# One slot later for the second projection, two conversion pieces at other slots, and differences one step ahead, in a two-layer MLP kernel on one Trainium2 core

## Chip, core and metric

The kernel runs on one core of one Trainium2 chip. The metric is the device time of one execution in microseconds; a kernel's time is the median of its runs. The engines are PE (TensorE; its weight loads are listed apart as PEld), DVE (VectorE), ACT (ScalarE), POOL (GpSimd) and SP (SyncE, which here issues nearly all DMAs).

## What is computed

Attention with random features gives `x` of 2304 tokens by 512 features. Two MLP layers follow, each 512 to 2048 to 512 in fp32:

```python
# layer 1
h = x @ w_in
g = h - np.tanh(h)
x = (g @ w_out)
# layer 2
h = x @ w_in
g = h * (1.0 / (1.0 + np.exp(-1.702 * h)))
out = (g @ w_out)
```

Weights arrive as 64-bit floats, and the kernel converts them itself. Every fp32 operand of a product is split into a high part and a low part (`two`: ACT casts `hi`, then POOL or DVE subtracts to get `lo`), and a product is three passes, hi·hi, hi·lo, lo·hi.

## The kernel before

The program has three stages: attention (with the first conversions of layer 1's weights), layer 1, and layer 2. All engines work through their instructions in program order, so the order in which the source emits instructions is the schedule.

**Layer 2** (from line 848 on) is cut into 24 groups: three blocks of 768 tokens (`sb` 0, 1, 2) by eight weight pairs `j`. `GROUPS` runs blocks 0 and 1 alternately over j = 0 to 7 (groups 0 to 15), then block 2 over j = 7 to 0 (groups 16 to 23). The first product of a group is done with seven products instead of eight, over sums and differences of 2x2 blocks: seven prepared forms of x (`xform`, P1 to P7) times seven prepared forms of the weights (`win`). Their results accumulate in PSUM banks: `a` (P1, P6, P5, P3 in this order), `c` (P7, P4) and `b` (P2). Between the products of a bank, `vec` copies or adds what the bank holds at that moment: `h_add` (line 864) makes `hx` on DVE, `keep` (line 868) a copy on ACT. So P6 in slot 2 can't start before the `hx` of G11, issued in slot 0, has read bank `a`.

A group has seven slots. In each slot PE gets one of the first products (`h_slot`; 6 matmuls) and one or two pieces of the second projection of the group before (`y_chunk`; 6 matmuls each, eight pieces (t, d) per group, placed by `YS`). A piece needs all of `g` for its half t of the tokens: G11 and G21 for t = 0, G12 and G22 for t = 1. `g` is made by ACT (sigmoid), DVE (multiply), ACT (cast to hi) and POOL (lo, line 886). `y_chunk` ends with a DVE addition into `yacc` (line 847), which stands on DVE's queue ahead of the slot's `vec` work.

**Conversion in layer 2.** For the pairs j = 3 to 7, groups 4 to 13 also convert weights. A pair takes two groups (an even and an odd one), and `L2_TICKS` says at which slot of which a piece runs: `a`, `b`, `c`, `d` convert a raw tile (two ACT instructions, then the DVE instructions of lines 289 and 294), `b`, `c`, `d` also split an earlier part into hi and lo on ACT and POOL; `s` makes four sums on DVE (line 451); `h`, `o`, `e` split on ACT and POOL.

**Forms of x.** `xprep_ticks` prepares the seven forms of a block in the order P2, P1, P7, P6, P4, P5, P3, in steps k = 0 to 6 for both halves kt. Steps 1 to 4 start with a difference on DVE (line 526), then `two` casts the source on ACT and subtracts on POOL (kt = 0) or DVE (kt = 1). Block 0 is prepared during layer 1, block 1 in groups 0 and 1, block 2 in groups 14 and 15.

**Layer 1** runs 36 steps per half of its hidden features; `y` lives in four PSUM banks which `evac` (line 402) adds up on DVE at the end of a token block, and the next block's `y_mm` waits for that.

Of the kernel before, what the change touches and what calls it, by code (L numbers as in the profile page):

```python
# [15 lines left out]
ALU = mybir.AluOpType  # L16
# [30 lines left out]
NPAIR = NF // 2  # L47
NPRE = 3
GROUPS = [(sb, j) for j in range(NPAIR) for sb in range(2)] + [(2, j) for j in reversed(range(NPAIR))]
NG = len(GROUPS)  # L50

L1_TICKS = ("a", "b", "s", "ch", "d", "oe")
L2_TICKS = {(0, 1): "a", (0, 5): "b", (0, 6): "s", (1, 1): "c", (1, 3): "h", (1, 5): "d", (1, 6): "o", (2, 0): "e"}
SLOTS = ("P1", "P7", "P6", "P4", "P5", "P2", "P3")
XID = dict(P2=0, P1=1, P7=2, P6=3, P4=4, P5=5, P3=6)
WID = dict(P1=0, P2=1, P7=2, P6=3, P5=4, P3=5, P4=6)
# [3 lines left out]
def body(ctx, tc, qT, kT, v, om, w1, w2, out):  # L60
    nc = tc.nc
# [445 lines left out]
    def xprep_ticks(sb, tiles, place):  # L507
        xi = {}

        def load():  # L510
            u = tiles(4)
            for kt in range(2):
                b1, b2 = tiles(2 * kt), tiles(2 * kt + 1)
                xi[kt] = b1, b2, u[:, kt, :]
                for i in range(2):
                    nc.sync.dma_start(
                        out=(b1, b2)[i],
                        in_=ysf[2 * i + kt, :, sb * 2 * TW:(sb + 1) * 2 * TW].rearrange("p (a c) -> p a c", c=TW))

        def tick(kt, k):  # L520
            b1, b2, t1 = xi[kt]
            b11, b12, b21, b22 = b1[:, 0, :], b1[:, 1, :], b2[:, 0, :], b2[:, 1, :]
            sums = {1: (t1, b12, b11), 2: (b12, b22, b12), 3: (b11, b22, t1), 4: (b21, b21, b11)}
            if k in sums:
                o, x, y = sums[k]
                nc.vector.tensor_tensor(out=o, in0=x, in1=y, op=ALU.subtract)
            src, i = ((b21, "P2"), (b11, "P1"), (b12, "P7"), (b11, "P6"), (b21, "P4"), (t1, "P5"), (b22, "P3"))[k]
            i = XID[i]
            v = place(i)[:, kt] if place else rp.tile([128, 2, TW], F32R, tag="xo", name="xo", bufs=4)
            two(v[:, 0, :], v[:, 1, :], src, (nc.gpsimd, nc.vector)[kt])  # L530
            if not place:
                store(xf[i, :, kt * 2 * TW:(kt + 1) * 2 * TW].rearrange("p (a c) -> p a c", c=TW), v.bitcast(F32))

        return load, [lambda kt=kt, k=k: tick(kt, k) for k in range(7) for kt in range(2)]

# [316 lines left out]
    def ya_tile(name):  # L852
        return l2.tile([128, 2, TW], F32, tag="yacc", name=name, bufs=8)

    YS = (((0, 0),), ((0, 1),), ((0, 2),), ((0, 3), (1, 0)), ((1, 1),), ((1, 2),), ((1, 3),))

    hx, sv, sg, gt = {}, {}, {}, {}

# [84 lines left out]
    for n in range(NG + 1):  # L943
        sb, j = GROUPS[min(n, NG - 1)]
        for s in range(7):
            flush()
            if n < NG and (n or s > 1):
                h_slot(n, s)
            if n:
                for t, d in YS[s]:  # L950
                    y_chunk(n - 1, t, d)
            if n < NG or s < 2:
                vec(n, s)
            if n == 0 and s == 1:
                evac(*ev, 0)
                load_win(1)
                load_wout(1)
            if n == NG:
                continue
            if s == 0 and n > 1:  # L960
                if sb == 0 and 1 <= j < NPAIR - 1:
                    (load_win if j + 1 < NPRE else new_w)(j + 1)
                elif sb == 2 and 0 < j < NPAIR - 1:
                    load_win(j - 1)
            if s == 6 and n > 1:
                if sb == 0 and 1 <= j < NPAIR - 1:
                    (load_wout if j + 1 < NPRE else new_wo)(j + 1)
                elif sb == 2 and 0 < j < NPAIR - 1:
                    load_wout(j - 1)
            q = n * 7 + s  # L970
            if xticks:
                if 3 <= q < 98 or q > 100:
                    xticks.popleft()()
                    xticks.popleft()()
            elif n == 1 and s == 4:
                begin, ts = conv_ticks(l2, range(NPRE, NPAIR), place)
                begin()
                ticks.extend(ts)
            if ticks:
                at = q - 7 * (2 * NPRE - 2)  # L980
                for x in L2_TICKS.get((at // 7 % 2, s), "") + (L2_TICKS.get((2, s), "") if at >= 14 and at // 7 % 2 == 0 else ""):
                    if at >= 0 and ticks[0][0] == x:
                        ticks.popleft()[1]()
            if n == 14 and s == 0:
                assert not ticks
                flush()

                def x2_tile(i):
                    if i == 4:
                        return l2.tile([128, 2, TW], F32, tag="ssum", name="xi", bufs=1)  # L990
                    return cv.tile([128, 2, TW], F32, tag=("raw", "ye")[i % 2], name="xi", bufs=2)

                xload, xt = xprep_ticks(2, x2_tile, lambda i: xform[2, i])
                xload()
                xticks.extend(xt)
                new_x2(2, 0)
            if n == 14:
                if SLOTS[s] != "P2":
                    new_x2(2, XID[SLOTS[s]])
# [48 lines left out]
```

## Time and profile before

| | us |
|---|---|
| median of 3 runs | 941.35 (939.5 to 942.11) |
| profiled execution, its own time | 941.45 |
| its span, first to last instruction | 939.7 |
| PE busy / PEld busy | 906.5 (96%) / 820.2 (87%) |
| DVE / ACT / POOL busy | 640.9 (68%) / 563.6 (60%) / 464.3 (49%) |

The profiled execution is 0.1 us above the median, and 1.75 us of it lie outside its span. A row of a timeline gives the start, the time from start to end, engine, source line, operation, tiles, and in brackets how long the engine was idle before it and what ended that. PE rows overlap, since matmuls are pipelined.

### The profile page before, as it was taken

How to read it: one execution, taken by the hardware profiler on the slowest of the kernel's cores; microseconds unless marked ns; L12 is line 12 of the kernel's file. 1: busy time of each engine (PE TensorE's matmuls, PEld its weight loads, DVE VectorE, ACT ScalarE, POOL GpSimd, SP SyncE). 2: the span in 40 equal slices, each digit the busy share in tenths (PEclk: the TensorE clock that was granted, in tenths of full speed). 3: DMA queues.
4: the chain of work that ended last, by engine and by line, in shares of the span. 5: the costliest groups of instructions: out<-in, count | busy, mean ns of one | idle time of the engine just before them, and what ended most of it. 6: DMA issues, size and time to landing. Idle time of an engine off the chain costs nothing.

```text
span 939.7 us, 14423 instructions
## 1 busy us (share of the span) xinstructions
PE 906.5 (96%) x5192; PEld 820.2 (87%) x5192; DVE 640.9 (68%) x1041; ACT 563.6 (60%) x1175; POOL 464.3 (49%) x361
## 2 busy tenths in 40 slices
PE   8999999999999999999989989999999998999998
PEld 6888877888898888888878879989989988999998
DVE  5999988756666656778656385577787777544454
ACT  5888878777777767777556453355554554333332
POOL 3555534556656656776746352244454565222222
PEclk9999999999999999999999999999999999999999
DMA  6787854033354242668655863034533111353542
GB/s 208 230 263 245 261 189 160 23 135 101 103 201 131 93 135 83 228 230 321 229 208 211 349 258 123 1 114 144 168 124 121 59 51 43 114 197 149 221 152 84
DMA packets 56248, 151.83 MB, mean 162 GB/s; under 512 B 6384, under 2 KB 13168, under 8 KB 53872
## 3 DMA queue, kind: packets, MB, share of 16 engines
q1 hardware_dynamic: 56032, 150.57, 46.7%
q8 instruction: 41, 0.67, 0.3%
q10 hardware_dynamic: 144, 0.33, 0.1%
q14 instruction: 31, 0.25, 0.1%
HBM read 104.48 MB, written 46.40 MB: 161 GB/s over the span
## 4 chain that ended last, share of the span: by engine, by line
PE 71%; DVE 12%; ACT 6%; POOL 5%; issue 4%; DMA 2%; SPq 0%; POOLq 0%; ACTq 0%; DVEq 0%
PE y L381 17%; PE hs L837 16%; PE hs L343 16%; PE y L816 13%; PE y L200 3%; PE y L183 2%; DVE raw L294 2%; PE y L124 1%; DVE ssum L451 1%; DVE yacc L847 1%; POOL wq L371 1%; DVE wq L373 1%; PE hs L152 1%; DVE hx L864 1%; DMA wfi<-stg 1%
## 5 line engine op out<-in xcount | busy, mean ns | idle before, releaser
L837 PE MATMUL hs<-g,wout 128*128 128x384 f32 x1152 | 229.1, 336 | 9.3 <-POOL g L886 8.5
L837 PEld LDWEIGHTS hs<-g,wout 128*128 128x128 f32 x1152 | 201.5, 188 | 13.4 <-POOL g L886 12.3
L343 PE MATMUL hs<-xb,w 128*128 128x512 f32 (+1 forms) x960 | 211.1, 371 | 1.5 <-DVE t L372 1.5
L816 PE MATMUL y<-x,win 128*128 128x384 f32 x966 | 195.0, 336 | 8.0 <-DVE hx L864 6.3
L381 PE MATMUL y<-ghi,w 128*128 128x512 f32 (+1 forms) x640 | 194.1, 371 | 4.3 <-DVE ye L402 4.3
L343 PEld LDWEIGHTS hs<-xb,w 128*128 128x128 f32 x960 | 168.6, 190 | 32.1 <-DVE t L372 1.7
L886 POOL TENSOR_TENSOR g<-sg,g 128x384 fp32r<-128x384 f32 x96 | 104.7, 1091 | 181.8 <-ACT g L885 177.0
L816 PEld LDWEIGHTS y<-x,win 128*128 128x128 f32 x966 | 169.4, 188 | 11.5 <-DVE hx L864 7.4
L357 POOL TENSOR_TENSOR glo<-wq,ghi 128x512 fp32r<-128x512 f32 x72 | 100.3, 1394 | 140.5 <-ACT ghi L355 140.5
L847 DVE TENSOR_TENSOR yacc<-hs,yacc 128x384 f32<-128x384 f32 x168 | 92.6, 554 | 100.0 <-PE hs L837 99.9
L373 DVE COPY_PREDICATED wq<-m,t 128x512 f32<-128x512 uint16 x72 | 86.1, 1196 | 106.1 <-POOL wq L371 105.0
L381 PEld LDWEIGHTS y<-ghi,w 128*128 128x128 f32 x640 | 117.9, 191 | 25.1 <-issue 5.2
L381 PE MATMUL y<-glo,w 128*128 128x512 f32 (+1 forms) x320 | 118.6, 371 | 0.0
L876 ACT ACTIVATE sg<-hx 128x384 f32<-128x384 f32 x72 | 37.8, 526 | 114.5 <-DVE hx L864 106.6
L885 ACT CAST g<-sg 128x384 fp32r<-128x384 f32 x96 | 49.4, 515 | 91.4 <-DVE sg L879 91.4
L371 POOL TENSOR_TENSOR wq<-wq,s 128x512 f32<-128x512 f32 x70 | 90.6, 1294 | 18.6 <-DVE wq L370 17.6
L134 POOL PARTITION_ALL_REDUCE mq<-pq x32 | 65.9, 2107 | 61.2 <-ACT pq L132 61.2
L363 ACT ACTIVATE s<-hs 128x512 f32<-128x512 f32 x72 | 42.9, 596 | 62.0 <-PE hs L343 61.9
L381 PEld LDWEIGHTS y<-glo,w 128*128 128x128 f32 x320 | 61.1, 191 | 10.0
L370 DVE SCALAR_TENSOR_TENSOR wq<-wq,hs 128x512 f32<-128x512 f32 x72 | 49.1, 682 | 18.6 <-ACT t L365 18.6
L355 ACT CAST ghi<-wq 128x512 fp32r<-128x512 f32 x72 | 44.3, 615 | 26.0 <-DVE wq L373 26.0
L364 ACT ACTIVATE wq<-s,qb 128x512 f32<-128x512 f32 x72 | 52.3, 726 | 7.2 <-POOL glo L357 0.6
(119 smaller groups left out, 1280.4 us busy)
## 6 DMA issues: line engine op xcount, KB each, us to landing
raw<-w SPq DMA_DIRECT2D x57, 512.0 KB, 4.4
xb<-xs SPq DMA_DIRECT2D x24, 512.0 KB, 5.6
win<-wfi SPq DMA_DIRECT2D x9, 1280.0 KB, 8.4
wout<-wfo SPq DMA_DIRECT2D x9, 1024.0 KB, 4.8
xf<-xo SPq DMA_DIRECT2D x14, 384.0 KB, 3.5
x<-xf SPq DMA_DIRECT2D x7, 768.0 KB, 12.3
vt<-v SPq DMA_DIRECT2D x16, 325.0 KB, 3.4
kt<-kT SPq DMA_DIRECT2D x15, 320.0 KB, 3.4
```

The source lines that it names most:

```text
L134: nc.gpsimd.partition_all_reduce(mqs[i, j], pq[:, j, :], channels=128, reduce_op=bass.bass_isa.ReduceOp.max)
L343: nc.tensor.matmul(h[:, j * n:j * n + n], w[:, 0, a, kt * 128:kt * 128 + 128], x[:, c, kt, :n], start=(k == 0), stop=(k == 11))
L357: nc.gpsimd.tensor_tensor(out=lo, in0=g, in1=hi.bitcast(F32), op=ALU.subtract)
L364: nc.scalar.activation(out=w, in_=s, func=AF.Square, scale=QS, bias=qb)
L371: (nc.vector if si < 2 else nc.gpsimd).tensor_tensor(out=w, in0=w, in1=s, op=ALU.mult)
L373: nc.vector.copy_predicated(out=w, mask=m.bitcast(mybir.dt.uint16), data=t)
L381: nc.tensor.matmul(y[d][:, :n], w[:, 1, a, d * 128:d * 128 + 128], g[c][:, j * n:j * n + n], start=(first and j == 0 and k == 0), stop=(la ...
L816: nc.tensor.matmul(dst, w[:, WID[name], a, kt * 128:kt * 128 + 128], xt[:, kt, c, :], start=(first and k == 0), stop=(k == 5), skip_group_ ...
L837: nc.tensor.matmul(dst, wout[j][:, f, a, d * 128:d * 128 + 128], gt[n, f, t][:, c, :], start=(k == 0), stop=(k == 5))
L847: nc.vector.tensor_tensor(out=u, in0=dst, in1=u, op=ALU.add)
L885: nc.scalar.copy(out=u[:, 0, :], in_=g)
L886: nc.gpsimd.tensor_tensor(out=u[:, 1, :], in0=g, in1=u[:, 0, :].bitcast(F32), op=ALU.subtract)
```

## The change

The pieces of the second projection move by one slot: an entry of `YS` now names how many groups back it works, so that slot 0 does the last piece of the group before the previous one, and slots 1 to 6 the other seven of the previous group. The load of `wout` moves with them from slot 6 to slot 0 of the next group. In `L2_TICKS`, `s` moves from slot 6 of the even group to slot 1 of the odd one, and `c` from slot 1 to slot 2. In `xprep_ticks` the difference that step k + 1 needs is made at the end of step k.

```diff
-L2_TICKS = {(0, 1): "a", (0, 5): "b", (0, 6): "s", (1, 1): "c", (1, 3): "h", (1, 5): "d", (1, 6): "o", (2, 0): "e"}
+L2_TICKS = {(0, 1): "a", (0, 5): "b", (1, 1): "s", (1, 2): "c", (1, 3): "h", (1, 5): "d", (1, 6): "o", (2, 0): "e"}
...
-            if k in sums:
-                o, x, y = sums[k]
-                nc.vector.tensor_tensor(out=o, in0=x, in1=y, op=ALU.subtract)
             src, i = ((b21, "P2"), (b11, "P1"), (b12, "P7"), (b11, "P6"), (b21, "P4"), (t1, "P5"), (b22, "P3"))[k]
...
+            if k + 1 in sums:
+                o, x, y = sums[k + 1]
+                nc.vector.tensor_tensor(out=o, in0=x, in1=y, op=ALU.subtract)
...
-    YS = (((0, 0),), ((0, 1),), ((0, 2),), ((0, 3), (1, 0)), ((1, 1),), ((1, 2),), ((1, 3),))
+    YS = (((2, 1, 3),), ((1, 0, 0),), ((1, 0, 1),), ((1, 0, 2), (1, 0, 3)), ((1, 1, 0),), ((1, 1, 1),), ((1, 1, 2),))
...
-            if n:
-                for t, d in YS[s]:
-                    y_chunk(n - 1, t, d)
+            for m, t, d in YS[s]:
+                if n >= m:
+                    y_chunk(n - m, t, d)
+            if n == NG and s == 6:
+                y_chunk(n - 1, 1, 3)
...
+            if s == 0 and n > 2:
+                at = GROUPS[n - 1]
+                if at[0] == 0 and 1 <= at[1] < NPAIR - 1:
+                    (load_wout if at[1] + 1 < NPRE else new_wo)(at[1] + 1)
+                elif at[0] == 2 and 0 < at[1] < NPAIR - 1:
+                    load_wout(at[1] - 1)
...
-            if s == 6 and n > 1:
-                if sb == 0 and 1 <= j < NPAIR - 1:
-                    (load_wout if j + 1 < NPRE else new_wo)(j + 1)
-                elif sb == 2 and 0 < j < NPAIR - 1:
-                    load_wout(j - 1)
```

**PE, the start of an odd group that converts** (L816 with `win` is a first product, two rows of L837 are one piece of the second projection; `g_6933` and `g_6998` are t = 0 of the group before, the other `g` are t = 1). Before:

```order
L816 MATMUL y_7011<-x_5597,win 128x384 x6
L837 MATMUL hs<-g_6933,wout 128x384 x3
L837 MATMUL hs<-g_6998,wout 128x384 x3
L816 MATMUL y_7032<-x_5598,win 128x384 x6
L837 MATMUL hs<-g_6933,wout 128x384 x3
L837 MATMUL hs<-g_6998,wout 128x384 x3
L816 MATMUL y_7011<-x_5599,win 128x384 x6
```

In the change the tiles are numbered anew: `g_6925` and `g_6990` are t = 0 of the group before, `g_6879` and `g_6851` t = 1 of the one before that.

```order
L816 MATMUL y_6995<-x_5597,win 128x384 x6
L837 MATMUL hs<-g_6879,wout 128x384 x3
L837 MATMUL hs<-g_6851,wout 128x384 x3
L816 MATMUL y_7017<-x_5598,win 128x384 x6
L837 MATMUL hs<-g_6925,wout 128x384 x3
L837 MATMUL hs<-g_6990,wout 128x384 x3
L816 MATMUL y_6995<-x_5599,win 128x384 x6
```

The first piece that reads the new t = 0 stands behind P7 instead of behind P1; between P1 and P6 there is one of its pieces, not two.

**DVE, from the end of an even group that converts into the odd one** (L289 and L294 belong to piece `b`, later ones to `c`; L451 is `s`; `hx<-..,sp` is G11 of the odd group). Before:

```order
L294 SCALAR_TENSOR_TENSOR raw_6380<-raw_6380 128x512
L847 TENSOR_TENSOR yacc<-hs,yacc 128x384
L879 TENSOR_TENSOR sg<-hx,sg 128x384
L451 TENSOR_TENSOR ssum<-raw_6380 128x256
L451 TENSOR_TENSOR ssum<-raw_6331,raw_6380 128x256
L451 TENSOR_TENSOR ssum<-ssum,raw_6331 128x256
L451 TENSOR_TENSOR ssum<-raw_6331,ssum 128x256
L847 TENSOR_TENSOR yacc<-hs,yacc 128x384
L864 TENSOR_TENSOR hx<-y_6672,sp 128x384
L879 TENSOR_TENSOR sg<-y_6502,sg 128x384
L847 TENSOR_TENSOR yacc<-hs,yacc 128x384
L289 SCALAR_TENSOR_TENSOR raw_6499<-raw_6499 128x512
```

In the change:

```order
L294 SCALAR_TENSOR_TENSOR raw_6389<-raw_6389 128x512
L847 TENSOR_TENSOR yacc<-hs,yacc 128x384
L880 TENSOR_TENSOR sg<-hx,sg 128x384
L847 TENSOR_TENSOR yacc<-hs,yacc 128x384
L865 TENSOR_TENSOR hx<-y_6656,sp 128x384
L880 TENSOR_TENSOR sg<-y_6494,sg 128x384
L847 TENSOR_TENSOR yacc<-hs,yacc 128x384
L451 TENSOR_TENSOR ssum<-raw_6389 128x256
L451 TENSOR_TENSOR ssum<-raw_6366,raw_6389 128x256
L451 TENSOR_TENSOR ssum<-ssum,raw_6366 128x256
L451 TENSOR_TENSOR ssum<-raw_6366,ssum 128x256
L847 TENSOR_TENSOR yacc<-hs,yacc 128x384
```

The four sums leave their place in front of `hx` and stand behind it, one slot on.

**DVE in layer 1, up to the addition that frees the PSUM banks of `y`** (L526 and L532 are the differences, L423 the low part of the x form for kt = 1). Before:

```order
L373 COPY_PREDICATED wq<-m,t 128x512 [waits DVE_49,Activation_49,Pool_49]
L526 TENSOR_TENSOR xi<-xi 128x384 x2
L423 TENSOR_TENSOR xo<-xi,xo 128x384 [waits DMAHW0_49,Activation_49]
L402 TENSOR_TENSOR ye<-y_4420,ye 128x512 [waits DMAHW7_49,PE_49]
L402 TENSOR_TENSOR ye<-y_4421,ye 128x512 [waits PE_49]
```

In the change:

```order
L373 COPY_PREDICATED wq<-m,t 128x512 [waits DVE_49,Activation_49,Pool_49]
L532 TENSOR_TENSOR xi<-xi 128x384
L423 TENSOR_TENSOR xo<-xi,xo 128x384 [waits DMAHW0_49,Activation_49]
L532 TENSOR_TENSOR xi<-xi 128x384
L402 TENSOR_TENSOR ye<-y_4420,ye 128x512 [waits DMAHW7_49,PE_49]
L402 TENSOR_TENSOR ye<-y_4421,ye 128x512 [waits PE_49]
```

The cast that L423 waits for no longer needs a difference of the same step; the two differences here are those of the step after.

## Rows read from the trace of the kernel before

**Rows 1.** PE in a stretch of windows (engines' busy us and counts, PEclk, DMA, GB/s)

```profile
800.00:926.00 126.00, 125.93 (x727) 125.61 (x726) 63.20 (x124) 41.96 (x90) 32.28 (x32) 1.00 0.41 158
```

**Rows 2.** Waits by engine, layer 2: us in total, times, longest

```profile
PE hs L837 <- POOL g L886: 8.5, 12, 1.0
...
PEld hs L837 <- POOL g L886: 12.3, 12, 1.3
```

**Rows 3.** The chain that ended last, in order of time: start us, us, what

```profile
604.81 1.04 PE y L816 x6
...
613.96 1.74 DVE raw L294
...
750.57 1.71 DVE raw L294
```

**Rows 4.** Timeline of PE in one pair of converting groups

```profile
615.05 0.86 PE L837 MATMUL hs<-g,wout 128*128 128x384 f32 x4
616.61 0.61 PE L837 MATMUL hs<-g,wout 128*128 128x384 f32 x2 [0.70 <-POOL g L886]
...
620.12 1.31 PE L816 MATMUL y<-x,win 128*128 128x384 f32 x6 [0.79 <-DVE hx L864]
...
634.18 0.62 PE L837 MATMUL hs<-g,wout 128*128 128x384 f32 x2 [0.62 <-POOL g L886]
```

**Rows 5.** Timeline of POOL at the same place

```profile
613.83 1.32 POOL L423 TENSOR_TENSOR win<-raw,win 128x512 fp32r<-128x512 f32 x1 [5.57 <-ACT win L422]
615.11 1.45 POOL L886 TENSOR_TENSOR g<-sg,g 128x384 fp32r<-128x384 f32 x1
...
621.54 1.02 POOL L886 TENSOR_TENSOR g<-sg,g 128x384 fp32r<-128x384 f32 x1 [2.69 <-ACT g L885]
```

**Rows 6.** Timeline of DVE at the same place

```profile
605.00 0.69 DVE L294 SCALAR_TENSOR_TENSOR raw<-raw 128x512 int32<-128x512 int32 x1
...
616.09 0.88 DVE L879 TENSOR_TENSOR sg<-hx,sg 128x384 f32<-128x384 f32 x1
616.89 0.41 DVE L451 TENSOR_TENSOR ssum<-raw 128x256 f32<-128x256 f32 x1
...
618.01 1.12 DVE L451 TENSOR_TENSOR ssum<-raw,ssum 128x256 f32<-128x256 f32 x1
...
619.52 0.54 DVE L864 TENSOR_TENSOR hx<-y,sp 128x384 f32<-128x384 f32 x1
```

**Rows 7.** Timeline of layer 1 where PE waits for the addition of `y`

```profile
470.55 0.98 ACT L422 CAST xo<-xi 128x384 fp32r<-128x384 f32 x2 [4.47 <-DVE xi L526]
...
477.11 1.01 DVE L526 TENSOR_TENSOR xi<-xi 128x384 f32<-128x384 f32 x2
...
479.60 2.47 DVE L402 TENSOR_TENSOR ye<-y,ye 128x512 f32<-128x512 f32 x4
...
480.43 0.36 PE L381 MATMUL y<-ghi,w 128*128 128x256 f32 x1 [4.33 <-DVE ye L402]
```

**Rows 8.** Windows around that wait and around a shorter one

```profile
476.00:484.00 8.00, 3.67 (x19) 3.60 (x19) 6.21 (x10) 3.81 (x7) 3.92 (x4) 0.80 0.22 79
...
550.00:556.00 6.00, 3.73 (x20) 3.34 (x20) 5.42 (x10) 1.50 (x4) 3.34 (x3) 1.00 1.01 376
```

**Rows 9.** Start of layer 2: its window, and a PE wait of the timeline

```profile
538.00:562.00 24.00, 19.72 (x102) 17.50 (x101) 19.83 (x30) 12.77 (x29) 13.00 (x12) 1.00 0.68 253
...
555.07 1.28 PE L816 MATMUL y<-x,win 128*128 128x384 f32 x6 [1.26 <-DVE hx L864]
```

**Rows 10.** Timeline of PE in groups 14 and 15

```profile
787.59 0.61 PE L837 MATMUL hs<-g,wout 128*128 128x384 f32 x2 [0.93 <-POOL g L886]
...
791.46 1.32 PE L816 MATMUL y<-x,win 128*128 128x384 f32 x6 [1.15 <-DVE hx L864]
```

**Rows 11.** SP's timeline in block 2, and the landing of `win` from its tile's view

```profile
835.08 0.32 SPq L714 DMA_DIRECT2D wout<-wfo  x1
835.45 0.90 SPq L708 DMA_DIRECT2D win<-wfi  x2
...
DMA to landing us min/median/max: 3.9/6.2/10.0
```

## The prediction

> **What bounds the kernel.** PE does, and the question is only where it still waits. The first view is the windows: in the late stretch of layer 2 PE and its weight loads are busy for all but a fraction of 126 us [rows 1], so nothing can be won there. The second view is the list of waits: over layer 2 PE waits twelve times for POOL's low part of g before a piece of the second projection [rows 2]. The third is the chain of waits in order of time. Where PE is not disturbed, six matmuls follow each other in 1.04 us [rows 3]; so a group of 7 first products and 8 pieces should take 15 x 1.04 = 15.6 us and a pair of groups 31.2. But in the stretch that converts weights the DVE instruction of line 294 recurs in the chain from 613.96 to 750.57 [rows 3], four pairs in 136.61 us, 34.15 each. So a converting pair loses 2.95 us.
>
> The timeline names the three places of that loss [rows 4]: the first piece of the second projection stops in the middle for the low part of G21 (616.61, and 634.18 in the next group), and P6 waits for hx (620.12). The same three repeat in all five pairs, fifteen waits. The other places where PE waits are one in layer 1 [rows 7], the start of layer 2 [rows 9], and groups 14 and 15 [rows 10]. A busier DVE costs nothing until PE waits for it.
>
> **How much one wait costs.** The rows of PE in one pair give 0.70 + 0.79 + 0.62 = 2.11 us idle [rows 4], while the period says 2.95. Over layer 2 the twelve waits are 8.5 us of idle PE but 12.3 us of idle weight loading [rows 2]: the PE rows carry modelled ends that cover part of the gap. I take the period, since it is elapsed time. The Trainium skill (Perfetto Trace Analysis, Identifying the Most-Contended Engine) calls matmul busy time a bad measure of distance to the bound, since matmuls are pipelined, and wants the weight loads' busy share; by PE's rows the five pairs would give 5 x 2.11 = 10.6 us, by the period 14.8. The trace sides with that page here.
>
> **Term 1, the converting groups.** *The low part of G21.* POOL works on a split of `win` (1.32 us) when the cast of G21 is ready, and its low part ends at 615.11 + 1.45 = 616.56 [rows 5]. The first piece started at 615.05 [rows 4] and ran four of six matmuls before it needed that. In the change P7 and a piece of older data come first: P1, old piece, P7, then the new piece at 615.05 + 2 x 1.04 = 617.13, which is past 616.56 before its first matmul. Both such waits of a pair go, and the pieces for t = 1 get a slot more as well. *P6 and hx.* Today the four sums run from 616.89 to 618.01 + 1.12 = 619.13, and hx comes after them, from 619.52 to 620.06 [rows 6]; P6 starts at 620.12. Without the sums the queue reads: multiplication until 616.97, one y addition (as long as the hx row, some 0.46 from start to start), hx from about 617.35 to 617.89. The old piece it adds ended at 615.05 + 1.04 = 616.09, so that addition is not late. P6 would be free to start at 615.05 + 3 x 1.04 = 618.17. It is met with 0.28 us to spare. *What is late next.* The sums (2.24 us) and the conversion of `c` (0.69 + 0.69 alone, 1.74 for the second where POOL is in the way [rows 3, 6]) now stand in slots 1 to 3 of the odd group, with four y additions, a multiplication and one hx at about 0.54: 6.9 to 7.9 us of DVE work in 7 x 1.04 = 7.28 us. DVE ends those slots at most 0.6 us late; the next product that waits for DVE is P3 in slot 6, two slots on, and the y pieces rotate through four PSUM buffers. ACT's casts and POOL's low parts behind the moved pieces keep a slot of room. So all three waits go: **5 x 2.95 = 14.8 us**. Ends: 14.8, and 7.4 if hx becomes a new wait (first rival).
>
> **Term 2, layer 1.** In one place PE stands 4.33 us for the addition of y (480.43), because DVE's queue has the x form in front: two differences at 477.11, then a low part that waits for ACT's cast, then the additions at 479.60 [rows 7]. ACT had waited 4.47 us for the differences a step earlier too (470.55) [rows 7], and the next step's activations stood behind that cast. With differences one step ahead the casts don't wait. Walking the queues on with row durations, the step before starts its activations some 3 us earlier, of which DVE's own work takes back a part, and the additions start near 477.0 instead of 479.6: **2.6 us**. Ends: 0.6 (only the last cast's wait goes) and 4.3. After the 4.33 us of idling the granted clock was at its lower level for a while: 0.80 on the mean of the 8 us around it, which is 0.2 x 8 = 1.6 us of full-clock work; after an idle time of 1.26 us it stayed at 1.00 [rows 8]. What remains of the wait, about 1.7 us, is nearer to the 1.26, so I count the **1.6 us** as won, with 0 as the low end.
>
> **Term 3, start of layer 2.** PE is busy 19.72 of 24 us there [rows 9], so 4.3 us can be won at most. But DVE is busy 19.83 of those 24 and works through the same differences, low parts and hx; they only change places, and one difference now stands before an hx of slot 4. P6 of group 1, which waited 1.26 us until 555.07 [rows 9], has one piece fewer before it and would start at some 553.9. That piece, 1.04 us, is done at the end of the kernel instead. Net **0.9 us**, ends -1 and 4.3.
>
> **Term 4, groups 14 and 15.** The wait for g at 787.59 (0.93) goes as in term 1. The wait for hx at 791.46 (1.15) [rows 10] shrinks little: the differences stay on DVE ahead of hx, only the stop for ACT's cast between them goes. I count **1.5 us**, ends 0 and 3.1.
>
> **At no cost.** The number of matmuls, DVE, ACT and POOL instructions and DMAs is unchanged. The last piece now follows after the loop, in a tail of PE work that is as long as what it left out earlier. The `wout` load is issued a slot later, behind a piece of slot 0, and `win` of the same slot behind it on SP; PE's cover for it is priced as the last rival. The `s` and `c` pieces issue their loads of raw weights one slot later; these are read seven slots on.
>
> Sum: 14.8 + 2.6 + 1.6 + 0.9 + 1.5 = 21.4 us, from the profiled execution's own 941.45 (its median stands 0.1 lower): **920.0 us**.
>
> **Rivals.**
>
> *hx is a new wait (chance 0.13).* The margin of 0.28 us in term 1 is the thinnest in the change. Line 294 took 0.69 us where POOL was idle and 1.74 us begun beside a POOL split [rows 3, 5, 6]. If one more low part of g, 1.02 us [rows 5], falls before hx at each of the ten group starts, each loses 1.02 - 0.28 = 0.74 us, 7.4 in all: 927.4 us. For it speaks that the moved pieces meet other POOL work than now; against it, that the instructions ahead of hx are the ones that stand there today, with their delays in my numbers. The Trainium skill (SBUF — State Buffer, Who interferes with whom) says that a DVE instruction with two SBUF inputs and a GpSimd one that reads SBUF exclude each other for the whole instruction, whichever came first; by that rule this rival is what happens wherever the two meet ahead of hx. The trace agrees with it at 613.96.
>
> *Everything goes (0.10).* The upper ends of all terms: 14.8 + 4.3 + 1.6 + 4.3 + 3.1 = 28.1 us, 913.4 us. Against it stands DVE's load at the start of layer 2.
>
> *Nothing comes of it (0.04).* The waits return elsewhere, since `g` is as late as before and only its reader moved: within 0.3% (2.8 us, about what a measurement can tell) of 941.4. A reader that moves by two products, 2.08 us, against waits of at most 1.3 us [rows 2] speaks against it.
>
> *Slower: the weights of block 2 come late (0.03).* `wout` now waits for the piece of slot 0 and `win` stands behind it on SP. Today both go at 835.08 and 835.45 [rows 11]; the change puts `win` at about 837.5. It must be there for P2 in slot 5, at 835.0 + 11 x 1.04 = 846.4. The slowest landing, 10.0 us [rows 11], would give 848, but that is the larger second part, which is read two slots later still. From 846.4 on each us late costs PE one us in each of six groups; to eat 21.4 us and 3 more, the load must be 4 us late in all six, a landing of 13 us, and the time would be above 944. No row shows such a landing.
>
> **How the numbers follow.** Forecast 0.70. The range takes in the forecast with the ends of its terms, the first rival and the second: 912 to 930. Outside are the last two rivals and rest of the tails. Faster by over 0.3%: 0.70 + 0.13 + 0.10 = 0.93; within: 0.04; slower: 0.03.
>
> **What would show it.** Right: no wait of PE on POOL's g in the converting groups, a pair's period near 31.2 us, the layer 1 wait under 2.6 us with a clock of 1.00 after it, no wait in block 2. Wrong: fifteen waits of about a us at other lines, or P6 waiting for hx in most converting groups; a wait of 4 us left in layer 1; PE waiting on `win` after 835.

## The result and the profile after

The changed kernel takes 933.68 us (median of 4 runs, 932.13 to 933.95), the kernel before 941.73 (4 runs, 939.5 to 942.5): ratio 0.9915, 95% interval 0.9895 to 0.9935. It is faster by some 8 us, where 21.4 were forecast, and lies above the upper end of the range (930). The profiled execution took 933.93 us with a span of 932.1, against 939.7 before.

The account below (7.6 us, against 7.5 between the spans) is taken between starts of the same matmuls in both traces (in layer 2 what is left after 0.1733 us, a sixth of 1.04, for each matmul of the stretch, since one piece of the second projection has moved from its start to its end).

| stretch | forecast, us won | measured, us won |
|---|---|---|
| up to layer 1's wait | 0 | -0.6 |
| layer 1's wait and the rest of layer 1 | 4.2 | -1.1 |
| start of layer 2 (groups 0 and 1) | 0.9 | -4.3 |
| converting groups 4 to 13, and group 14 | 14.8 | 13.1 |
| group 15 | 1.5 | 0.5 |
| rest | 0 | 0.0 |
| sum | 21.4 | 7.6 |

Group 14 stands with the converting groups because the fifteenth of the waits that the prediction counted there is in its slot 0. The first row is chance: in both traces the 16 matmuls of line 152 that start at 5.64 us run the same code, and take 2.08 us here and 1.50 before; over the runs below the same 16 take 1.16 to 2.08.

**The converting groups did what was forecast.** In the page's group of the second projection PE no longer waits for `g` (the 12 waits of [rows 2] are gone):

```profile
L837 PE MATMUL hs<-g,wout 128*128 128x384 f32 x1152 | 226.2, 335 | 0.0
```

In the chain of waits (start us, us, what) the same work of a pair now recurs every 31.54 us, (737.06 - 610.90) / 4, where it was 34.15 [rows 3]; 31.2 was forecast:

```profile
610.90 2.08 PE hs L837 x12
...
737.06 2.08 PE hs L837 x12
```

What is left is one short stop of P6 for `hx` at the start of groups 6, 8, 10, 12 and 14, 0.26 us each (0.52 in group 10). In group 6 two sixes of matmuls take 640.12 - 637.78 = 2.34 instead of 2.08. PE's timeline, and DVE's with what stands ahead of that `hx` (the last instruction of a converted piece, 1.67 us beside a POOL split, and a multiplication of 0.90):

```profile
637.78 1.21 PE L837 MATMUL hs<-g,wout 128*128 128x384 f32 x6
638.97 1.31 PE L816 MATMUL y<-x,win 128*128 128x384 f32 x6
640.12 1.20 PE L837 MATMUL hs<-g,wout 128*128 128x384 f32 x6
```

```profile
635.02 1.67 DVE L294 SCALAR_TENSOR_TENSOR raw<-raw 128x512 int32<-128x512 int32 x1
...
637.09 0.90 DVE L880 TENSOR_TENSOR sg<-hx,sg 128x384 f32<-128x384 f32 x1
...
638.37 0.54 DVE L865 TENSOR_TENSOR hx<-y,sp 128x384 f32<-128x384 f32 x1
```

**The waits that are left** (PE; us in total, times, longest) stand in layer 1 and at the start of layer 2, and they have grown:

```profile
PE y L381 <- DVE ye L402: 5.2, 1, 5.2
PE y L816 <- ACT x L422: 2.9, 1, 2.9
PE y L816 <- DVE hx L865: 2.8, 2, 2.6
```

The first was 4.33 [rows 7]. The second is P6 of group 1; it was 1.26 [rows 9]. The view names ACT's cast there, because it ended last by the profile, but the timeline shows `hx` ending at that moment (557.29 + 0.54 = 557.83, PE starts at 557.98). The 2.6 of the third line is in group 15.

**Layer 1.** DVE's timeline ahead of the additions of `y`, then POOL's:

```profile
477.28 1.50 DVE L373 COPY_PREDICATED wq<-m,t 128x512 f32<-128x512 uint16 x1 [0.86 <-POOL wq L371]
478.68 0.54 DVE L532 TENSOR_TENSOR xi<-xi 128x384 f32<-128x384 f32 x1
479.14 0.54 DVE L423 TENSOR_TENSOR xo<-xi,xo 128x384 fp32r<-128x384 f32 x1
479.61 1.61 DVE L532 TENSOR_TENSOR xi<-xi 128x384 f32<-128x384 f32 x1
481.15 2.47 DVE L402 TENSOR_TENSOR ye<-y,ye 128x512 f32<-128x512 f32 x4
```

```profile
477.20 0.99 POOL L423 TENSOR_TENSOR xo<-xi,xo 128x384 fp32r<-128x384 f32 x1
479.51 1.30 POOL L357 TENSOR_TENSOR glo<-wq,ghi 128x512 fp32r<-128x512 f32 x1 [1.31 <-ACT ghi L355]
```

The casts do not hold DVE up any more, as intended. But the predicated copy now starts 0.08 us after a POOL subtraction and takes 1.50 us, and the second difference starts 0.10 us after another and takes 1.61 instead of 0.54. So the additions start at 481.15 instead of 479.60 [rows 7]; 0.6 of that is the first row of the table, and 0.9 is the growth of the wait.

Such instructions had two durations before as well. DVE's timeline there, the predicated copy three steps ahead of the additions, a low part, and the copy of the last step:

```profile
458.38 1.55 DVE L373 COPY_PREDICATED wq<-m,t 128x512 f32<-128x512 uint16 x1 [2.52 <-POOL wq L371]
...
465.63 1.64 DVE L423 TENSOR_TENSOR xo<-xi,xo 128x384 fp32r<-128x384 f32 x1
...
476.49 0.73 DVE L373 COPY_PREDICATED wq<-m,t 128x512 f32<-128x512 uint16 x1 [1.83 <-POOL wq L371]
```

Over the whole kernel the same 24 differences cost DVE 22.4 us instead of 13.3 (groups of lines; busy, mean ns). Before, and then after:

```profile
L526 DVE TENSOR_TENSOR xi<-xi 128x384 f32<-128x384 f32 x24 | 13.3, 595 | 0.0
```

```profile
L532 DVE TENSOR_TENSOR xi<-xi 128x384 f32<-128x384 f32 x24 | 22.4, 933 | 0.0
```

**Start of layer 2.** DVE's timeline, POOL's, and PE's:

```profile
552.06 1.35 DVE L423 TENSOR_TENSOR x<-xi,x 128x384 fp32r<-128x384 f32 x1
553.34 1.36 DVE L532 TENSOR_TENSOR xi<-xi 128x384 f32<-128x384 f32 x1
...
556.02 1.34 DVE L532 TENSOR_TENSOR xi<-xi 128x384 f32<-128x384 f32 x1
557.29 0.54 DVE L865 TENSOR_TENSOR hx<-y,sp 128x384 f32<-128x384 f32 x1
```

```profile
551.68 1.32 POOL L887 TENSOR_TENSOR g<-sg,g 128x384 fp32r<-128x384 f32 x1
552.96 1.32 POOL L423 TENSOR_TENSOR x<-xi,x 128x384 fp32r<-128x384 f32 x1
555.79 1.17 POOL L887 TENSOR_TENSOR g<-sg,g 128x384 fp32r<-128x384 f32 x1 [1.50 <-ACT g L886]
```

```profile
557.98 2.26 PE L816 MATMUL y<-x,win 128*128 128x384 f32 x6 [2.85 <-ACT x L422]
```

A difference or a low part that meets a POOL subtraction takes 1.35 us here, and POOL's own take 1.32 instead of 1.02. Four of the eight differences from 545 to 557 us are held so, and all eight stand ahead of `hx`. The `hx` itself, with one of its two inputs in PSUM, takes 0.54 although POOL runs another subtraction from 556.91 to 558.23. The windows (busy us and counts of PE, PEld, DVE, ACT, POOL; PEclk) show what the wait then cost beyond itself:

```profile
538.00:562.00 24.00, 18.14 (x82) 15.73 (x81) 18.23 (x26) 12.53 (x28) 12.61 (x11) 0.90 0.69 260
...
561.00:563.00 2.00, 2.00 (x8) 2.00 (x8) 0.80 (x2) 0.58 (x2) 1.56 (x2) 0.50 0.04 8
```

PE is busy 1.58 us less than before (18.14 against 19.72 [rows 9]), and it then works at the lower of its two clock levels (0.50, 1.2 of 2.4 GHz) until some 564.0: from 557.98 that is 6.0 us, in which half as much is done, 3.0 us. Together 4.6, about the 4.3 of the table. Block 2 has no waits, as before [rows 1]: PE is again busy 125.93 of the 126 us from 800 on.

### The profile page after: what moved, and what is told of

Same layout as the page of the kernel before. It is cut to its first block, busy times and chain, and to the rows that moved or that the text cites. A ratio compares the mean times of both kernels' runs of the same rounds, so it can differ in the third digit from the quotient of the medians.

```text
span 932.1 us, 14425 instructions
## 1 busy us (share of the span) xinstructions
PE 906.5 (97%) x5192; PEld 823.8 (88%) x5192; DVE 650.5 (70%) x1041; ACT 564.5 (61%) x1175; POOL 465.8 (50%) x361
## 4 chain that ended last, share of the span: by engine, by line
PE 76%; DVE 12%; POOL 4%; issue 3%; ACT 3%; DMA 1%; SPq 0%; POOLq 0%; ACTq 0%; DVEq 0%
PE hs L837 19%; PE y L816 16%; PE y L381 16%; PE hs L343 15%; PE y L200 3%; DVE xi L532 2%; PE y L183 2%; POOL wq L371 2%; PE y L124 1%; DVE wq L373 1%; DVE raw L294 1%; PE hs L152 1%; DMA wfi<-stg 1%; POOL mq L134 1%; DVE yacc L847 1%
## 5 line engine op out<-in xcount | busy, mean ns | idle before, releaser
L837 PE MATMUL hs<-g,wout 128*128 128x384 f32 x1152 | 226.2, 335 | 0.0
L816 PE MATMUL y<-x,win 128*128 128x384 f32 x966 | 196.8, 338 | 7.8 <-ACT x L422 2.9
L837 PEld LDWEIGHTS hs<-g,wout 128*128 128x128 f32 x1152 | 203.0, 189 | 0.0
L816 PEld LDWEIGHTS y<-x,win 128*128 128x128 f32 x966 | 170.8, 189 | 11.2 <-DVE hx L865 5.1
L294 DVE SCALAR_TENSOR_TENSOR raw<-raw 128x512 int32<-128x512 int32 x57 | 56.8, 996 | 1.6
```

What stands on the lines that cost most here:

```text
L294: nc.vector.scalar_tensor_tensor(out=c, in0=c, scalar=3, in1=z, op0=ALU.logical_shift_left, op1=ALU.bitwise_or)
L816: nc.tensor.matmul(dst, w[:, WID[name], a, kt * 128:kt * 128 + 128], xt[:, kt, c, :], start=(first and k == 0), stop=(k == 5), skip_group_ ...
L837: nc.tensor.matmul(dst, wout[j][:, f, a, d * 128:d * 128 + 128], gt[n, f, t][:, c, :], start=(k == 0), stop=(k == 5))
```

## The experiments

Twelve runs in three rounds, each timed against the kernel before in the same round (941.28, 941.51, 941.56 us). The first four take the change apart.

**e1_late_diff**: the change, with the differences back at the head of their own step.

```diff
+            if k in sums:
+                o, x, y = sums[k]
+                nc.vector.tensor_tensor(out=o, in0=x, in1=y, op=ALU.subtract)
...
-            if k + 1 in sums:
-                o, x, y = sums[k + 1]
-                nc.vector.tensor_tensor(out=o, in0=x, in1=y, op=ALU.subtract)
```

> The changed kernel with the differences back in their own step; y pieces and conversion pieces stay moved. Theory D (the early differences are what costs: as third DVE instruction of a step they meet a POOL split and take 1.35 to 1.65 us instead of 0.54): 926 us, the layer 1 wait back to 4.3 us, no half clock after group 1's P6 at the start of layer 2, the conversion stretch as in the change. Rival S (the missing y piece in slot 0 of group 1 is what leaves PE idle and cold at the start of layer 2): 931 us, the half clock there stays.

929.48 us, ratio 0.9868 (0.9855 to 0.9881): 4.2 faster than the change. The wait in layer 1 is 4.29 again, the converting groups keep their gain, and the start of layer 2 loses 1.5 us against before, where the change loses 4.3. So the early differences are a loss. But the time lies between the two theories (926 and 931), and theory D missed at the start of layer 2: P6 of group 1 waits 2.56 us there with late differences too, and the clock falls behind it (0.57 and 0.58 in the windows from 556 to 560):

```profile
555.16 1.32 PE L816 MATMUL y<-x,win 128*128 128x384 f32 x6 [2.56 <-DVE hx L865]
```

So part of the loss there comes from the moved piece: P6 has one piece fewer ahead of it and stands longer for an `hx` that comes no more than half a microsecond earlier.

**e2_early_diff_alone**: before, with the opposite edit.

> The kernel before with the differences one step ahead and nothing else. Theory D: slower than before by 4 to 6 us (946 us), a layer 1 wait of about 5.2 us, and at the start of layer 2 the differences at 1.35 us and more waits of PE. Rival S: within 1.5 us of before (941 to 943).

945.03 us, ratio 1.0038 (1.0026 to 1.0051), 3.8 slower. The wait in layer 1 is 5.23 and P6 of group 1 waits 2.68 for `hx`. The third part of the change, alone, costs about what e1 gave back (theory D said 4 to 6), though not at the same places: the start of layer 2 loses 1.0 us here, where e1 gave back 2.8, and the clock stays at 1.00 there in spite of the wait of 2.68.

**e3_y_shift_alone**: before, with the new `YS` and `wout` at its new slot.

```diff
-    YS = (((0, 0),), ((0, 1),), ((0, 2),), ((0, 3), (1, 0)), ((1, 1),), ((1, 2),), ((1, 3),))
+    YS = (((2, 1, 3),), ((1, 0, 0),), ((1, 0, 1),), ((1, 0, 2), (1, 0, 3)), ((1, 1, 0),), ((1, 1, 1),), ((1, 1, 2),))
```

> The kernel before with the y pieces one slot later and nothing else. The low part of G21 no longer stops PE, but the four sums still stand ahead of hx, which then ends at the same place while P6 is free about 1 us sooner: of 2.95 us per converting pair only about 0.7 is won. Theory C (both moves are needed, each wait hides behind the other): 936 us. Rival I (the two moves are independent and add, two waits in three go): 930 us.

942.88 us, ratio 1.0011 (1.0 to 1.0021): nothing won. PE's timeline in two of the five pairs:

```profile
654.79 1.72 PE L816 MATMUL y<-x,win 128*128 128x384 f32 x6 [1.79 <-DVE hx L865]
656.31 2.12 PE L837 MATMUL hs<-g,wout 128*128 128x384 f32 x6
...
689.65 1.32 PE L816 MATMUL y<-x,win 128*128 128x384 f32 x6 [1.79 <-DVE hx L865]
690.82 1.21 PE L837 MATMUL hs<-g,wout 128*128 128x384 f32 x6
```

The waits for G21 are gone, and PE arrives that much earlier at P6, where the sums still hold `hx` back: 1.8 us at one place instead of 0.70, 0.79 and 0.62 at three. In four of the five pairs the lower clock follows that stop (six matmuls in 2.12 us), in the third it does not (1.21). Between the same matmuls the third pair wins 0.9 us, about what theory C had (0.7), and each of the others loses 0.7. So both theories missed the time, and what theory C left out is the clock; the fastest of the 11 runs, with a granted clock of 0.995 where the others have 0.987 or 0.989, took 938.03.

**e4_pieces_alone**: before, with `s` and `c` at their new slots.

```diff
-L2_TICKS = {(0, 1): "a", (0, 5): "b", (0, 6): "s", (1, 1): "c", ...
+L2_TICKS = {(0, 1): "a", (0, 5): "b", (1, 1): "s", (1, 2): "c", ...
```

> The kernel before with the conversion pieces s and c at their new slots and nothing else. hx is no longer behind the sums, the two waits per pair for the low part of G21 stay: about 1 us per pair is won. Theory C and rival I both: 936 to 937 us; below 932 would say that the sums also delayed the low part of G21.

938.14 us, ratio 0.9963 (0.9951 to 0.9975). The waits for `hx` in the converting groups are gone, those for G21 stay:

```profile
PE hs L837 <- POOL g L886: 10.6, 12, 1.1
```

The time is 1.1 us above what both theories said. So neither of the two moves wins the 13.1 us. Alone they give -1.6 and 3.1 (by e3's fastest run, 938.03, the first would be 3.3); the two belong together.

**The second round** asked why the early differences lose.

**e5_early_diff_lo_on_dve**: the change, with every low part of an x form on DVE, none on POOL.

```diff
-            two(v[:, 0, :], v[:, 1, :], src, (nc.gpsimd, nc.vector)[kt])
+            two(v[:, 0, :], v[:, 1, :], src, nc.vector)
```

> The changed kernel with the low parts of the x forms of kt = 0 on DVE instead of POOL, so that POOL has seven instructions less to collide with in each of the three preparations. Theory X (DVE and POOL exclude each other where DVE reads two SBUF operands; the early differences cost because they meet these low parts and the splits of g): although DVE gets seven instructions more, fewer of its differences take 1.35 us, PE's waits at the start of layer 2 shrink by 2 us or more and the layer 1 wait falls below 4.3: 929 us or less. Rival Q (DVE is simply full there): seven more instructions of 0.54 make it later, 935 us or more.

929.08 us, ratio 0.987 (0.9855 to 0.9886), at the edge of theory X: 4.6 faster than the change, though DVE does more. The wait in layer 1 is 3.98, and at the start of layer 2, up to 553.6 us, nearly every DVE instruction takes 0.54 or 0.55. But POOL's low parts of `g` are then held up by a row of DVE instructions without a gap, here three of 1.02, and PE waits for them:

```profile
549.20 7.61 POOL L887 TENSOR_TENSOR g<-sg,g 128x384 fp32r<-128x384 f32 x3 [5.25 <-ACT g L886]
```

```profile
553.71 1.01 PE L837 MATMUL hs<-g,wout 128*128 128x384 f32 x2 [2.36 <-POOL g L887]
```

**e6_late_diff_lo_on_dve**: the same edit on e1.

> The same with the differences back in their own step (the changed kernel otherwise). Theory X: every cast waits for its difference again, so the stop for ACT of 0.58 us stands twice per step; about as e1, 929 us, layer 1 wait 4.3 us or somewhat more. Rival Q: 933 us or more.

936.77 us, ratio 0.9952 (0.9939 to 0.9964), as the rival had it. With late differences DVE stops for a cast before each low part, and there are now two of them: the wait in layer 1 is 5.1, and one for `hx` in group 15 3.9. So it is not only the blocking: DVE's queue in front of the additions counts, whatever makes it long.

**e7_diff_at_start_of_step**: the change, with the early differences at the head of a step instead of its end.

```diff
+            if k + 1 in sums:
+                o, x, y = sums[k + 1]
+                nc.vector.tensor_tensor(out=o, in0=x, in1=y, op=ALU.subtract)
             src, i = ((b21, "P2"), (b11, "P1"), ...
...
-            if k + 1 in sums:
-                o, x, y = sums[k + 1]
-                nc.vector.tensor_tensor(out=o, in0=x, in1=y, op=ALU.subtract)
```

> The changed kernel with the difference for step k + 1 at the start of step k instead of its end: DVE does difference, difference, low part, as before the change, while the casts still need nothing of their own step. Theory X: the DVE instruction that stands third behind the predicated copy is blocked by POOL's split, whichever it is, so now the low part takes 1.6 us and the differences 0.54, and the additions that PE waits for end as late: layer 1 wait about 5.2 us, 933 us. Rival O (the order difference, low part, difference is what is bad): the layer 1 wait falls to 2 us or less, 928 us.

932.32 us, ratio 0.9907 (0.9894 to 0.992), and a wait of 5.27 in layer 1, as theory X had it. DVE's timeline in layer 1:

```profile
477.16 1.50 DVE L373 COPY_PREDICATED wq<-m,t 128x512 f32<-128x512 uint16 x1 [0.86 <-POOL wq L371]
478.56 1.01 DVE L526 TENSOR_TENSOR xi<-xi 128x384 f32<-128x384 f32 x2
479.49 1.61 DVE L423 TENSOR_TENSOR xo<-xi,xo 128x384 fp32r<-128x384 f32 x1
481.03 2.47 DVE L402 TENSOR_TENSOR ye<-y,ye 128x512 f32<-128x512 f32 x4
```

The two differences take 0.5 each here, and the low part that now stands third takes 1.61. It is the place in the queue that is hit: of these subtractions, all with both inputs in SBUF, the one that DVE starts while POOL splits `g` is held.

**e8_late_diff_wq_on_dve**: e6, with the product of `wq` (line 371) on DVE in the steps that prepare x.

```diff
-        (nc.vector if si < 2 else nc.gpsimd).tensor_tensor(out=w, in0=w, in1=s, op=ALU.mult)
+        (nc.vector if si < 2 or per + 22 <= si <= per + 28 else nc.gpsimd).tensor_tensor(out=w, in0=w, in1=s, op=ALU.mult)
```

> e6 with one more move in layer 1 only: in the seven steps that prepare x forms the product of wq and s (1.29 us on POOL) is on DVE. Theory X: it takes 0.55 us there when POOL is quiet, the loop of DVE and POOL that is longer than a step of PE gets shorter, and the layer 1 wait falls to 2.5 us or less: 2 to 4 us faster than e6. Rival Q: DVE later still, layer 1 wait 5 us or more.

934.13 us, ratio 0.9926 (0.9913 to 0.9938), 2.6 faster than e6, which is in theory X's 2 to 4. But the wait only fell from 5.1 to 4.5, not to 2.5: the reason missed. The chain through POOL's product is a small part of that wait.

**The third round** takes the work out of the queue instead of changing it. In layer 1 the step just before the additions issues no x form (the later ones move on by one step), and the forms of block 2 go out one half per slot instead of two.

```diff
-            elif xticks and sp > 21:
+            elif xticks and sp > 21 and sp != 25:
...
                     xticks.popleft()()
-                    xticks.popleft()()
+                    if n < 14:
+                        xticks.popleft()()
```

**e10_late_diff_free_queue**: e1 with these two edits.

> The change with its differences back in their own step, and two more edits: the step of layer 1 right before the additions of y issues no x form (the forms after it go one step later), and the forms of block 2 are issued one half per slot instead of two. Theory Q (each wait is as long as the x-form work that stands ahead on DVE's queue): the additions of y follow the predicated copy at once, the wait in layer 1 falls from 4.29 us to 1.7 to 2.2 us, the stretch at half clock behind it shrinks or goes, and the wait of 2.37 us for hx in group 14 or 15 falls under 1 us; the time is 923 to 926 us, against 929.5 with the late differences alone. Rival L (the wait in layer 1 is set by the chain of the activations, which run late step by step, and the forms only fill the time): the wait stays over 3.5 us, the time is 927 us or more, and what is won comes from groups 14 and 15 alone.

925.99 us, ratio 0.9839 (0.9826 to 0.9853): theory Q. The wait in layer 1 is 1.83, that in group 15 is gone.

**e13_late_diff_free_queue_spread**: e10, with the last forms of block 1 spread too.

```diff
-                    if n < 14:
+                    if q < 8 or q == 10:
```

> As the first run of this call, and of the forms of block 1 the last three steps are spread too: two halves per slot up to the fourth step, then two, one, one and two. Theory Q: P6 of group 1 waits for hx behind the forms issued before slot 0 of group 1, which this does not change, so its wait of about 2.5 us stays and only the small waits around it can go: 0 to 1 us faster than the first run of this call. Rival: the forms issued after slot 0 matter as well, and the wait falls under 1.5 us, 1.5 us or more faster.

925.93 us, ratio 0.9836 (0.9822 to 0.9849), as theory Q had it: P6 of group 1 still waits 2.58 us for `hx`. These two runs share their code up to layer 2, and show one thing more. Both wait 1.83 us in layer 1, but after it e10 fell to the lower clock and e13 did not. The window, and the next wait of PE for the additions, first of e10, then of e13 (window and timeline in turn):

```profile
480.00:482.00 2.00, 2.00 (x11) 2.00 (x10) 1.16 (x2) 0.00 (x0) 1.28 (x1) 0.50 1.01 371
```

```profile
503.66 0.47 PE L381 MATMUL y<-ghi,w 128*128 128x512 f32 x1 [1.15 <-DVE ye L402]
```

```profile
480.00:482.00 2.00, 2.00 (x16) 1.87 (x16) 1.17 (x2) 0.00 (x0) 1.28 (x1) 1.00 0.82 304
```

```profile
503.64 0.47 PE L381 MATMUL y<-ghi,w 128*128 128x512 f32 x1 [2.59 <-DVE ye L402]
```

PE goes on at 503.65 in both: 1.4 us won by the clock were handed on to the next wait.

**e11_early_diff_free_queue**: the change itself with the two edits.

> The change itself (early differences) with the same two edits. Theory Q: the wait in layer 1 falls from 5.24 us to about 2 us, with less time at half clock behind it, the wait of 2.60 us in group 14 falls under 1 us, and the start of layer 2 stays as it is with the change (four waits, one near 2.9 us): 925 to 928 us. The price of the early differences is then left in the start of layer 2 alone, 2 to 4 us above the run with late differences of this call. Rival L: the wait in layer 1 stays over 4.5 us, 930 us or more.

922.91 us, ratio 0.9803 (0.9789 to 0.9818). DVE's and PE's timelines in layer 1:

```profile
477.24 0.73 DVE L373 COPY_PREDICATED wq<-m,t 128x512 f32<-128x512 uint16 x1 [0.86 <-POOL wq L371]
477.86 2.48 DVE L402 TENSOR_TENSOR ye<-y,ye 128x512 f32<-128x512 f32 x4
```

```profile
478.68 0.36 PE L381 MATMUL y<-ghi,w 128*128 128x256 f32 x1 [1.92 <-ACT ghi L355]
```

The wait falls from 5.24 to 1.92, as theory Q had it, and the time is 2 us lower than it said. The price it put on the early differences against e10 (2 to 4 us) was wrong: by medians e11 is 3.1 faster. Its profiled execution was the slowest of five (925.92, the lowest 921.57) and does not show that difference: its span, 924.1, is that of e10, and its clock fell after the 1.92 us:

```profile
480.00:482.00 2.00, 2.00 (x11) 2.00 (x11) 1.53 (x3) 1.76 (x4) 0.93 (x1) 0.50 0.86 320
```

**e12_early_diff_free_queue_lo_on_dve**: e11, with the low parts of x for blocks 0 and 1, and of `g` for group 0, on DVE.

```diff
-            two(v[:, 0, :], v[:, 1, :], src, (nc.gpsimd, nc.vector)[kt])
+            two(v[:, 0, :], v[:, 1, :], src, nc.vector if kt or sb < 2 else nc.gpsimd)
...
-        nc.gpsimd.tensor_tensor(out=u[:, 1, :], in0=g, in1=u[:, 0, :].bitcast(F32), op=ALU.subtract)
+        (nc.vector if n == 0 else nc.gpsimd).tensor_tensor(out=u[:, 1, :], in0=g, in1=u[:, 0, :].bitcast(F32), op=ALU.subtract)
```

> As the run before, with the low parts of the x forms of blocks 0 and 1 all on DVE, and the low part of g of group 0 on DVE too, so that no POOL split of x or g stands against DVE's work at the start of layer 2. Theory B (what the start of layer 2 loses with early differences is DVE and POOL blocking each other): the DVE instructions with two inputs in SBUF take 0.54 us there, none over 1 us, POOL is not held for several us, and the start loses no more than with late differences: 922 to 925 us. Rival D (DVE has more work there than its time, wherever blocking falls): PE still waits 4 us or more in all at the start, 926 us or more.

920.70 us (4 runs, 920.4 to 921.08), ratio 0.9781 (0.9767 to 0.9794): it beats both kernels, the change by 13 us. DVE's and PE's timelines in layer 1, the window behind the wait, and P6 of group 1:

```profile
476.07 0.73 DVE L373 COPY_PREDICATED wq<-m,t 128x512 f32<-128x512 uint16 x1 [0.87 <-POOL wq L371]
476.70 2.47 DVE L402 TENSOR_TENSOR ye<-y,ye 128x512 f32<-128x512 f32 x4
```

```profile
477.52 0.35 PE L381 MATMUL y<-ghi,w 128*128 128x256 f32 x1 [1.04 <-ACT ghi L355]
...
549.16 1.69 PE L816 MATMUL y<-x,win 128*128 128x384 f32 x6 [1.81 <-ACT x L422]
```

```profile
480.00:482.00 2.00, 2.00 (x13) 1.74 (x12) 1.14 (x3) 0.69 (x2) 1.20 (x1) 1.00 0.77 286
```

All DVE instructions of the forms take 0.55 at the start of layer 2, and POOL is idle there until 554.46. The start loses 0.6 us against before, where e11 loses 3.2 and the change 4.3: theory B, with a time 1.3 us below its range. In layer 1 the same matmuls take 4.9 us less than before, where e11 wins 2.6.

## Why the prediction was wrong, step by step

**Term 1 (converting groups) was right in its mechanism**, and 1.7 us too large: 13.1 instead of 14.8. Between the same matmuls groups 4 to 14 had lost 14.75 us before, five times 2.95, so the period was the right measure. All fifteen waits went as forecast, and five short ones for `hx` took their place (the row at 638.97), 1.6 us in all. They stand at the even starts, where PE had stopped 0.62 us for `g` [rows 4] and so came late enough for `hx`; I had walked that queue for the odd start only. The first rival, a new wait on `hx`, thus came with 0.26 us once in a pair instead of 0.74 twice. e3 and e4 show that the term is one thing and not a sum of two.

**Term 2 (layer 1) failed, and with it the sign.** The step that failed reads: "Walking the queues on with row durations, ... the additions start near 477.0 instead of 479.6". They started at 481.15, 0.6 of it by chance. The walk took away the stops for ACT's casts and went by the durations of the last two steps [rows 7], where the copy and the differences met no POOL subtraction. A change that lets DVE run without stopping puts its instructions beside POOL's subtractions: in each of the four steps the predicated copy takes 1.50 to 1.54 and the second difference 1.61 to 1.65. That eats what the stops had cost. From the copy at 459.03 to the one at 477.28 three steps take 18.25 us; before, from 458.38 to 476.49, they took 18.11; PE needs three times 5.62 (its products of x start at 462.46, 468.08 and 473.70). In the last step, 3.87 us pass from the copy's start to the additions, 3.11 before, although the stop for the cast (0.58) is gone, since the copy grew by 0.77 and a difference by 1.07. The two together are the 0.9 us by which the wait grew. The long durations were in the trace of before, two and three steps ahead of the additions (1.64 at 465.63, 1.55 at 458.38). The Trainium skill (SBUF — State Buffer, Who interferes with whom), which says that a DVE instruction with two SBUF inputs and a GpSimd one that reads SBUF exclude each other for the whole instruction, was in my text, but weighed against one wait in layer 2 only, and given 7.4 us and a chance of 0.13. The traces agree with it: in e12 such instructions take 0.55 with POOL idle, in the change and in e7 1.34 to 1.65 beside it. The rule bore on terms 2 and 3, where I let it out. My low end for this term, 0.6 us won, excluded a loss without a reason.

**The clock part of term 2** said: "What remains of the wait, about 1.7 us, is nearer to the 1.26, so I count the 1.6 us as won". No such short wait came of it in the change, but the third round made one: after 1.83 the clock fell in e10 and held in e13, after 1.92 it fell, after 1.04 it held. So 1.7 was not on the safe side. In e12, with 1.04 left and the clock at 1.00, layer 1 won 4.9 us where the term said 4.2: the gain was there, and what the change lacked for it was the step without forms ahead of the additions (e11) and the low parts on DVE (e12).

**Term 3 (start of layer 2) failed in the same step, and in one more.** The first is "they only change places": four differences took some 1.35 instead of 0.54 ahead of the one `hx` that P6 waits for; alone, in e2, the early differences lose 1.0 us there. The second is that P6 "would start at some 553.9", one piece earlier: P6 waits for `hx` and not for the piece. In e3, with the pieces moved and the differences late, it starts at 554.88 after 2.58 us of waiting, and the stretch loses 0.6 instead of winning 0.9. The rest of the 4.3 is the lower clock, about 3 us, which followed the wait of 2.85 in the change and did not follow 2.68 in e2 or 2.58 in e3. The low end of -1 left these out. What e12 shows is that the forms can have their place with almost no loss, if POOL does not stand against them.

**Term 4** came to 0.5 instead of 1.5: a wait of 2.60 for `hx` took the place of 0.93 and 1.15. I had counted a removed wait for `g` as won, without asking that PE arrives earlier at the next. e10 to e13 show what was to be had there: with the forms spread the wait is gone, and group 15 wins 2.8 to 3.3 us.

The last rival, weights of block 2 late, did not occur: PE is busy 125.93 of 126 us, as before [rows 1]. That the early differences alone make the kernel slower by 3.8 us, shown in e2, was no rival of mine.

**Left open.** Why the first 16 matmuls of line 152 take 1.16 to 2.08 us from one execution to another is not shown. In which stretch e11 gains its 3.1 us on e10 is not shown by their traces. Why P6 of group 1 keeps a wait of 1.8 us in the best version was not tried; the lower clock follows it there too. Which of two executions with the same wait falls to the lower clock is not settled.

## What to carry to other kernels

A wait that is taken away is won only if the next thing PE needs is ready that much earlier; cost a change at the wait that comes after, and expect two moves to win together what neither wins alone. When an engine is freed of its stops, ask what it will now run beside: durations read where DVE and POOL took turns do not hold where they overlap, and any DVE instruction with two inputs in SBUF has then to be priced at both values. In front of an instruction on which PE waits, an empty stretch of queue was worth more here than earlier or faster work in it.

## What the hardware showed that was not expected

- The predicated copy is blocked as well: 0.73 us alone, 1.50 to 1.54 beside a POOL subtraction in each of the last four steps of the change, and 1.55 already before (458.38).
- The blocking goes both ways and can starve POOL: three subtractions of 1.02 us took 7.61 while DVE ran two-input instructions back to back (e5). In e12 they are on DVE too, with x's low parts, and it is 2.2 us faster than e11.
- TensorE's clock is not a matter of the wait's length alone: it fell after 1.83 us in e10 and held after 1.83 in e13; in e3 it fell after 1.77 to 1.79 in four pairs and held after 1.79 in the fifth; and in the change it held through a wait of 2.60 in group 15, behind which the six matmuls took 1.31:

```profile
783.59 1.31 PE L816 MATMUL y<-x,win 128*128 128x384 f32 x6 [2.60 <-DVE hx L865]
```
